# Attention with pooled keys and a channel mix on one core: probabilities transposed in 32 by 32 blocks on VectorE and moved through device memory

## The chip, the core and the metric

One core of one Trainium2 chip runs the whole kernel in one launch. The core has TensorE (PE, matrix products, with weight loads listed apart as PEld), VectorE (DVE), ScalarE (ACT), GpSimd (POOL) and SyncE (SP, which here only issues transfers). The metric is the device time of one launch in microseconds; smaller is better.

## The reference

```python
# attention: q, k, v are [8, 8, 576, 64]; keys and values are means over groups of 8
k_p = k.reshape(B, H, Sp, pool, D).mean(axis=3)          # Sp = 72
v_p = v.reshape(B, H, Sp, pool, D).mean(axis=3)
scores = scale * np.matmul(q, k_p.transpose(0, 1, 3, 2))
scores = scores - np.max(scores, axis=-1, keepdims=True)
attn = np.exp(scores)
attn = attn / (np.sum(attn, axis=-1, keepdims=True) + 1e-09)
x = np.matmul(attn, v_p)       # then heads side by side: x is [8, 576, 512]
# channel mix
x_prev = np.concatenate([np.zeros((B, 1, D)), x[:, :-1, :]], axis=1)   # D = 512
xk = mu_k * x + (1.0 - mu_k) * x_prev
xr = mu_r * x + (1.0 - mu_r) * x_prev
k = np.maximum(xk @ w_k, 0.0)                            # w_k [512, 1024]
v = k * k @ w_v                                          # w_v [1024, 512]
r = 1.0 / (1.0 + np.exp(-(xr @ w_r)))                    # w_r [512, 512]
return r * v
```

All is float32, and the result is [8, 576, 512].

## The kernel before

The 8 x 576 = 4608 tokens are cut into 12 chunks of 384 and each chunk into three tiles of 128, 36 tiles in all. A batch is one and a half chunks. Every part of the work is a Python generator (a thread): `softmax(i)` for a tile, `transposed(i)` and `transposed_rest(c, first, n)` for the transposes of its probabilities, `attended(c, g, p)` for the product with the values of head pair g (four pairs), `x_parts` for the split of the mixed inputs, `hidden(c, jt, p)` for eight blocks of the first product, `gate(c, tt)` and `mixed(c, tt)` for three tiles of the other two.

From chunk 1 on products are made of three products of split operands: each operand is rounded to a shorter type (its high part, names ending in h) and the difference is kept as a low part (ending in l); high times high, low times high and high times low are added. In chunk 0 weights and inputs are used whole. The weights arrive with eight bytes per number, in `got_wk`, `got_wr` and `got_wv` (eight, four and eight blocks of 512 KB), and `convert` makes 32-bit numbers of them: L510 on ScalarE, then a pass for the last bits, L513 on ScalarE or L518 on VectorE as `LAST_BITS_BY` says, then L523 and L526 on VectorE. `split` (L539 on ScalarE, L542 on VectorE or GpSimd by `LOW_BY`) makes the parts for the chunks behind the first.

A tile's probabilities go this way: scores of two heads at a time (L670, bank `sc`, 128 tokens by 8 heads by 72 keys); row maximum (L685); subtraction and exponential (L703, L708, sum in L710), or for the tiles of `BY_HEAD` eight exponentials with a bias and a running sum (L694); division as a product with a reciprocal, the first 64 keys of each head into `pm` (L728) and the last 8 into `px` (L722), on VectorE or GpSimd by `NORM_BY`. TensorE then transposes `pm` in four pieces (L747) and `px` in one (L774); ScalarE and VectorE copy the results out of the banks as `pth`, `ptl` and `ptr` (L755, L758, L760, L782, L785, L791). `attended` multiplies (L833). ScalarE scales the product into `t` (L840), GpSimd carries the token before a chunk (L847, L849, L851), VectorE mixes (L860, `xm`), ScalarE rounds (L876: `xkh`, `xrh`) and GpSimd subtracts (L878: `xkl`, `xrl`). Then come `hidden` (L905 and the squares L917 to L932), `gate` (L956, L963) and `mixed` (L988, L1002), and the output (L1004).

The order of the instructions is made before the run: class `Order` steps through all threads, keeps for each engine the time at which it is free by a table of costs, and of the threads whose next step could start takes the one with the smallest due time. Due times come from formulas (`FIRST`, `PER_TOKEN`, `tile_due`, `att_due`) and, where the table `DUE` names a thread, from that. Each engine then runs its own list in that order, and waits where an operand or a buffer isn't ready. All transfers but one are in SyncE's list.

`SUM_BY` says who adds the eight members of a group: "v" VectorE and "g" GpSimd by halving (L550), "t" TensorE by eight matmuls with the identity (L561, `summed`).

Of the kernel before, what the change touches and what calls it, by code (L numbers as in the profile page):

```python
# [21 lines left out]
KM = 64  # L22
# [19 lines left out]
    "k1 k0 q0 wk1 q1 v0 q2 wk5 v1 c0 v2 k3 wk0 r0 wr3 k2 wk2 wk7 q5 q3 wk6 v3 wv7 q4 wk4 wk3 "  # L42
    "wv6 wv3 wr1 r1 wv1 wv4 wv2 wv0 wr2 wv5 wr0 "
)

SUM_BY = {"k0": "v", "k1": "v", "v0": "v", "v1": "t", "r0": "t", "k2": "t", "k3": "v", "v2": "g", "v3": "g", "r1": "g", "k5": "g", "k4": "v", "v5": "v", "r2": "g", "v4": "g"}

NORM_BY = {0: "v", 1: "g", 2: "v", 3: "v", 7: "v", 5: "g", 4: "g", 8: "g", 6: "g"}
# [3 lines left out]
LAST_BITS_BY = {"k": "aaaaavaa", "r": "aava", "v": "aaaavaav"}  # L52
LOW_BY = {"k": "vgvgvvvv", "r": "vvgv", "v": "gvvvggvg"}
BY_HEAD = (0, 1, 5, 6)
# [2 lines left out]
SQUARED_ON_ACT = 7
# [1045 lines left out]
```

## Time and profile before

| | us |
|---|---|
| median of 3 runs (lowest, highest) | 641.22 (638.55, 642.38) |
| profiled execution, its own time | 642.0 |
| its span, first to last instruction | 640.1 |
| TensorE busy | 618.4 (97%), 3188 matmul records |
| VectorE, ScalarE, GpSimd busy | 380.7, 371.8, 211.2 |
| granted TensorE clock, mean | 0.99 |
| moved by DMA | 50.91 MB |

Busy times are unions over the span; lines of the form L905 are lines of the kernel before. In the rows below, `x704` counts records, the two numbers behind the bar are busy microseconds and mean nanoseconds of one record, and what follows the second bar is idle time of the engine ahead of them and what ended it. A float32 matmul of whole operands shows as two records. Records of TensorE overlap, so the time of a run of matmuls is read from the chain of work, not from the mean. A row of windows names a stretch, its length, the busy time of PE, PEld, DVE, ACT and POOL with counts, the granted clock, the share of the DMA engines and GB/s.

### The profile page before, as it was taken

The page shows a single profiled execution, that of the slowest core. Times are in us where ns is not written, and L with a number is a line of the kernel's source. Part 1 is how long each engine was busy: PE and PEld are TensorE (multiplying, and loading weights), DVE is VectorE, ACT ScalarE, POOL GpSimd, SP SyncE. Part 2 cuts the span into 40 slices and gives each one's busy share as a digit, 9 for nine tenths or more (in the row PEclk, how much of TensorE's full clock was granted, in tenths as well). Part 3 has the DMA queues.
Part 4 walks back from the last instruction along what each step waited for, and adds up shares of the span by engine and source line. Part 5 has one row for each costly group of instructions (what it writes and reads, how often), then busy time and mean ns, then how long its engine had stood idle before and what let it go on. Part 6 is the DMA issues. An engine that isn't in the chain of part 4 may idle for free.

```text
span 640.1 us, 8886 instructions
## 1 busy us (share of the span) xinstructions
PE 618.4 (97%) x3188; PEld 534.3 (83%) x3188; DVE 380.7 (59%) x723; ACT 371.8 (58%) x761; POOL 211.2 (33%) x327
## 2 busy tenths in 40 slices
PE   5898988999999999999999999999999999999997
...
GB/s 315 356 355 91 123 39 103 34 112 135 1 33 50 1 198 65 18 93 138 17 17 54 30 180 51 34 18 33 141 107 50 34 2 33 17 1 33 17 1 50
DMA packets 35132, 50.91 MB, mean 80 GB/s; under 512 B 6544, under 2 KB 23184, under 8 KB 35088
## 3 DMA queue, kind: packets, MB, share of 16 engines
...
q10 hardware_dynamic: 144, 0.13, 0.1%
...
## 4 chain that ended last, share of the span: by engine, by line
PE 83%; ACT 2%; POOL 0%; DVE 0%; issue 0%; DVEq 0%
PE mm L905 29%; PE mm L988 28%; PE mm L956 14%; PE bank L833 5%; PE sc L670 4%; PE bank L747 2%; ACT t L840 1%; PE bank L774 1%; ACT e L694 0%; POOL xkl L878 0%; ACT L694 0%; ACT got_wv L513 0%; ACT w_k L539 0%; ACT kbd L586 0%; POOL xrl L878 0%
## 5 line engine op out<-in xcount | busy, mean ns | idle before, releaser
L905 PE MATMUL mm<-xkh,w_k 128*128 128x384 f32 x704 | 181.6, 338 | 0.0
L988 PE MATMUL mm<-w_v,sh 128*128 128x512 f32 x528 | 171.1, 393 | 0.0
L905 PEld LDWEIGHTS mm<-xkh,w_k 128*128 128x128 f32 x704 | 126.0, 188 | 1.6 <-issue 1.4
L905 PE MATMUL mm<-xkl,w_k 128*128 128x384 f32 x352 | 117.9, 335 | 1.6 <-POOL xkl L878 1.6
L988 PEld LDWEIGHTS mm<-w_v,sh 128*128 128x128 f32 x528 | 99.2, 188 | 19.5
L988 PE MATMUL mm<-w_v,sl 128*128 128x512 f32 x264 | 102.9, 390 | 0.0
L956 PE MATMUL mm<-w_r,xrh 128*128 128x512 f32 x264 | 86.2, 397 | 0.0
L840 ACT ACTIVATE t<-bank,om_sb 128x384 f32<-128x384 f32 x96 | 49.1, 583 | 55.9 <-PE bank L833 55.2
L860 DVE SCALAR_TENSOR_TENSOR xm<-bank,mu_sb,t 128x384 f32<-128x384 f32 x88 | 50.7, 614 | 48.6 <-POOL t L851 26.1
L722 POOL TENSOR_TENSOR px<-e,sm 128x64 f32<-128x64 f32 x32 | 10.6, 332 | 203.5 <-DVE sm L716 198.0
L930 ACT CAST sh<-rk 128x384 fp32r<-128x384 f32 x88 | 45.1, 514 | 45.3 <-DVE rk L924 44.3
L905 PEld LDWEIGHTS mm<-xkl,w_k 128*128 128x128 f32 x352 | 66.1, 188 | 1.9 <-POOL xkl L878 1.9
L932 DVE TENSOR_TENSOR sl<-rk,sh 128x384 fp32r<-128x384 f32 x88 | 53.1, 608 | 23.7 <-ACT sh L930 22.9
L917 ACT ACTIVATE rk<-mm 128x384 f32<-128x384 f32 x88 | 43.0, 488 | 35.8 <-PE mm L905 33.8
L1002 DVE TENSOR_TENSOR rs<-mm,rs 128x512 f32<-128x512 f32 (+1 forms) x37 | 24.9, 674 | 63.2 <-PE mm L988 63.0
L924 DVE SCALAR_TENSOR_TENSOR rk<-mm,rk 128x384 f32<-128x384 f32 x88 | 48.6, 554 | 23.0 <-ACT rk L917 22.6
L550 POOL TENSOR_TENSOR stage<-stage 128x512 f32<-128x512 f32 (+8 forms) x60 | 52.5, 888 | 24.6 <-DMA stage<-in_kT 10.4
L878 POOL TENSOR_TENSOR xkl<-xm,xkh 128x384 fp32r<-128x384 f32 x44 | 44.9, 1022 | 45.1 <-ACT xkh L876 44.7
L956 PEld LDWEIGHTS mm<-w_r,xrh 128*128 128x128 f32 x264 | 49.6, 188 | 9.9
L988 PEld LDWEIGHTS mm<-w_v,sl 128*128 128x128 f32 x264 | 49.7, 188 | 8.9
L956 PE MATMUL mm<-w_r,xrl 128*128 128x512 f32 x132 | 51.4, 390 | 0.0
L670 PE MATMUL sc<-kbd,qs 128*128 128x144 f32 (+1 forms) x312 | 41.5, 292 | 5.9 <-ACT kbd L586 3.3
...
## 6 DMA issues: line engine op xcount, KB each, us to landing
out<-rs SPq DMA_DIRECT2D x35, 256.0 KB, 2.0
...
qs<-in_qT SPq DMA_DIRECT2D x32, 256.0 KB, 3.2
...
```

Of the source, the lines that this page charges most:

```text
L550: nc_eng.tensor_tensor(out=st[:, :, :w], in0=st[:, :, :w], in1=st[:, :, w:2 * w], op=ALU.add)
L670: nc.tensor.matmul(out=halves[g // 2][o:o + n, 0, k:k + 2 * KEYS], lhsT=qs[:, g, o:o + n], rhs=kbd[b % 2][:, g, :], start=True, stop=True,)
L840: nc.scalar.activation(out=t[:, m, 1:n + 1], in_=xp, func=AF.Copy, scale=om_sb[:, m, g:g + 1])
L860: nc.vector.scalar_tensor_tensor(out=xm[:, :n], in0=xp, scalar=mu_sb[:, m, g:g + 1], in1=t[:, m, :n], op0=ALU.mult, op1=ALU.add,)
L878: nc.gpsimd.tensor_tensor(out=lo, in0=xm[:, :n], in1=hi, op=ALU.subtract)
L905: nc.tensor.matmul(out=hp, lhsT=w[:, o], rhs=x[:, ct, o_t], start=(ct == 0 and k == 0), stop=(ct == NCT - 1 and k == len(terms) - 1),)
L917: nc.scalar.activation(out=rk[:, :n], in_=hp, func=AF.Relu)
L924: nc.vector.scalar_tensor_tensor(out=rk[:, :n], in0=hp, scalar=0.0, in1=rk[:, :n], op0=ALU.max, op1=ALU.mult)
L930: nc.scalar.copy(out=sh, in_=rk[:, :n])
L932: nc.vector.tensor_tensor(out=operand("sl", c)[:, jt, o_t], in0=rk[:, :n], in1=sh, op=ALU.subtract)
L956: nc.tensor.matmul(out=bank, lhsT=x[:, ct, o], rhs=w, start=(ct == 0 and k == 0), stop=(ct == NCT - 1 and k == len(terms) - 1),)
L988: nc.tensor.matmul(out=bank, lhsT=s[:, o], rhs=w, start=(jt == 0 and k == 0), stop=(jt == NJT - 1 and k == len(terms) - 1),)
```

## The change

For the tiles of chunks 2 to 11 the transposes on TensorE are gone. `softmax` normalizes all 72 keys in place (one pass), and a new thread `turned` has VectorE transpose the tile in blocks of 32 by 32 into `pm` (two instructions of 256 elements per partition and one of 64) and writes it to device memory (`passing`, two buffers of one chunk each). `fetch_turned` reads a chunk back in five transfers into `turned_sb` so that the blocks lie where whole transposes would have put them, and `split_turned` makes `pth`, `ptl` and `ptr` from it, out of SBUF instead of a bank. `turned_sb` is one buffer; until the weights are converted its space serves as the four temporaries of `convert` (two before).

The other tables are written anew as well: the order of the loads, who sums, who normalizes, which exponentials go by head, where the last bits of the weights are made (ScalarE 16 blocks of 20 before, 7 now), who makes the low parts, and all due times (two leads become constants `TILE_LEAD` and `ATT_LEAD`).

```diff
 LOADS = (
-    "k1 k0 q0 wk1 q1 v0 q2 wk5 v1 c0 v2 k3 wk0 r0 wr3 k2 wk2 wk7 q5 q3 wk6 v3 wv7 q4 wk4 wk3 "
-    "wv6 wv3 wr1 r1 wv1 wv4 wv2 wv0 wr2 wv5 wr0 "
+    "k0 q3 k1 v1 q0 wr3 q1 r0 c0 wk0 q4 wk1 q2 wv6 k3 v0 k2 wk4 wr2 wv1 wr0 wk3 wk2 v3 v2 wk5 "
+    "q5 wv2 wv4 r1 wk7 wv7 wv5 wk6 wv3 wv0 wr1 "
 )
-SUM_BY = {"k0": "v", "k1": "v", "v0": "v", "v1": "t", "r0": "t", "k2": "t", "k3": "v", "v2": "g", "v3": "g", "r1": "g", "k5": "g", "k4": "v", "v5": "v", "r2": "g", "v4": "g"}
-NORM_BY = {0: "v", 1: "g", 2: "v", 3: "v", 7: "v", 5: "g", 4: "g", 8: "g", 6: "g"}
+SUM_BY = {"k0": "t", "k1": "t", "v0": "t", "v1": "t", "r0": "t", "k2": "t", "k3": "t", "v2": "v", "v3": "g", "r1": "v", "k5": "v", "k4": "v", "v5": "v", "r2": "v", "v4": "v"}
+NORM_BY = {0: "g", 1: "g", 2: "v", 3: "g", 7: "v", 5: "v", 4: "g", 8: "v", 6: "v"}
-LAST_BITS_BY = {"k": "aaaaavaa", "r": "aava", "v": "aaaaavaav"}
-LOW_BY = {"k": "vgvgvvvv", "r": "vvgv", "v": "gvvvggvg"}
-BY_HEAD = (0, 1, 5, 6)
+LAST_BITS_BY = {"k": "aaavvavv", "r": "vavv", "v": "vavvvavv"}
+LOW_BY = {"k": "gvvvvvvv", "r": "vvvg", "v": "vgvvvgvv"}
+BY_HEAD = (0, 4, 8)
-SQUARED_ON_ACT = 7
+SQUARED_ON_ACT = 8
+TURNED = 2
+BLOCK = 32
 DUE = {
...
-    "attended 1 0 0": 8.52, "attended 1 1 0": 42.01, "attended 1 2 0": -16.71, "attended 1 3 0": -45.79,
+    "attended 1 0 0": -189.68, "attended 1 1 0": -34.56, "attended 1 2 0": -32.08, "attended 1 3 0": 49.09,
...
-PER_TOKEN = 0.131
+PER_TOKEN = 0.1331
+TILE_LEAD = -7.9807
+ATT_LEAD = 20.4607
...
-    slots("pm", 2, [P, 2, 4, KM])
+    slots("pm", 2, [P, 2 * 4 * KEYS])
...
-    slots("tmp", 2, [P, WP])
+    turned_sb = const.tile([P, CH // BLOCK, 6 * BLOCK], F32, name="turned_sb")
+    for i in range(4):
+        order.give("tmp", turned_sb.rearrange("p a n -> p (a n)")[:, i * WP:(i + 1) * WP])
+    passed = ctx.enter_context(tc.tile_pool(name="passed", bufs=1, space=bass.MemoryType.DRAM))
+    passing = [passed.tile([CH // P, P, 18 * BLOCK], F32, name=f"passing{i}") for i in range(2)]
...
-        begin[c - 1] + 5 + 0.042 * o if c > 1 else (begin[0] + SECOND + 0.03 * o if c else o / P) for c, o, _ in tiles
+        begin[c - 1] + TILE_LEAD + 0.042 * o if c > 1 else (begin[0] + SECOND + 0.03 * o if c else o / P) for c, o, _ in tiles
...
-    att_due = [b - 24 if c else 0 for c, b in enumerate(begin)]
+    att_due = [b - ATT_LEAD if c else 0 for c, b in enumerate(begin)]
...
         eng = nc.vector if v else nc.gpsimd
+        if tiles[i][0] >= TURNED:
+            yield dve(8 * KEYS) if v else pool(8 * KEYS)
+            eng.tensor_tensor(out=e, in0=e, in1=sm.broadcast_to([P, 2, 4, KEYS]), op=ALU.mult)
+            order.give("sm", sm)
+            yield from turned(i, e)
+            return
...
+    def turned(i, e):
+        c, off, _ = tiles[i]
+        u = yield take("pm")
+        yield "dve", 0.9, False
+        pairs = e.rearrange("p a (h two) k -> p (a h) two k", two=2)
+        for h2 in range(2):
+            nc.vector.transpose(
+                out=u[:, h2 * 8 * BLOCK:(h2 + 1) * 8 * BLOCK].rearrange("p (f g j) -> p f g j", f=2, j=BLOCK),
+                in_=pairs[:, :, h2, :KM].rearrange("p g (f j) -> p f g j", j=BLOCK),
+            )
+        nc.vector.transpose(
+            out=u[:, 16 * BLOCK:].rearrange("p (r h k) -> p r h k", r=2, k=KR), in_=e[:, :, :, KM:]
+        )
+        order.give("e", e)
+        if c - 2 >= TURNED:
+            yield need(("turned", c - 2))
+        yield "sp", 0.6, False
+        nc.sync.dma_start(out=passing[c % 2][off // P], in_=u)
+        order.fetched(("passed", i), 450)
...
+    def fetch_turned(c):
+        n = CHUNKS[c] // P
+        yield need(*[("passed", i) for i, t in enumerate(tiles) if t[0] == c])
+        d = yield take("turned")
+        yield "sp", 3.0, False
+        from_dram = passing[c % 2][:n].rearrange("t (a i) m -> i (t a) m", i=BLOCK)
+        for q in range(4):
+            nc.sync.dma_start(
+                out=d[q * BLOCK:(q + 1) * BLOCK, :n * 4, :4 * BLOCK],
+                in_=from_dram[:, :, q * 4 * BLOCK:(q + 1) * 4 * BLOCK],
+            )
+        nc.sync.dma_start(out=d[:BLOCK, :n * 4, 4 * BLOCK:], in_=from_dram[:, :, 16 * BLOCK:])
...
+    def split_turned(i):
+        c, off, _ = tiles[i]
+        yield need(("turned", c), ("attended", c - 1))
...
+        nc.scalar.copy(out=pt_h, in_=main)
+        nc.scalar.copy(out=ptr[:rows], in_=rest)
+        nc.vector.tensor_tensor(out=pt_l, in0=main, in1=pt_h, op=ALU.subtract)
+        nc.vector.tensor_tensor(out=ptr[rows:2 * rows], in0=rest, in1=ptr[:rows], op=ALU.subtract)
+        nc.scalar.copy(out=ptr[2 * rows:], in_=rest)
...
+        if tiles[i][0] >= TURNED:
+            order.add(tile_due[i] + 0.1, split_turned(i), spare)
+            continue
```

What stands where changes on every engine. Three places are shown. The first is TensorE where chunk 6 begins: the end of the last `mixed` tile of chunk 5 (weights `w_v`), the scores of a tile (`sc`), and `hidden` of chunk 6 (`w_k`). Before, the four matmuls of the last `attended` group stand 21 matmuls of `mixed` further up:

```order
L988 MATMUL mm_117<-w_v_759,sh_2492 128x512
L988 MATMUL mm_117<-w_v_759,sl_2527 128x512
L988 MATMUL mm_117<-w_v_759,sh_2492 128x512
L670 MATMUL sc_111<-kbd_69,qs_103 128x144 x4
L905 MATMUL mm_115<-xkh_2754,w_k_426 128x384 x2
L905 MATMUL mm_115<-xkl_2755,w_k_426 128x384
```

Now, on the same engine and at the same place, the last `attended` group (L932, the old L833) has moved behind `mixed`:

```order
L1087 MATMUL mm_118<-w_v_1024,sl_2575 128x512
L1087 MATMUL mm_118<-w_v_1024,sh_2538 128x512
L932 MATMUL bank_115<-pth_2662,vbd_h_71 128x384
L932 MATMUL bank_115<-pth_2662,vbd_l_73 128x384
L932 MATMUL bank_115<-ptl_2663,vbd_h_71 128x384
L932 MATMUL bank_115<-ptr_2664,vbd_r_75 128x384
L692 MATMUL sc_114<-kbd_70,qs_107 128x144 x4
L1004 MATMUL mm_120<-xkh_2814,w_k_490 128x384 x2
L1004 MATMUL mm_120<-xkl_2815,w_k_490 128x384
```

Behind these rows the first two blocks of `hidden` alternate: three quarters of the first, one quarter of the second, then the last quarter of the first, which is the first to use the group just shown.

The second place is SyncE's list in an even chunk: query loads (`qs`) and outputs (`out`), and before nothing else but the loads of keys and values:

```order
L1004 DMA out<-rs_78 128x512
L1004 DMA out<-rs_77 128x512
L1004 DMA out<-rs_79 128x512
L469 DMA qs_104<-in_qT 128x4x128
L469 DMA qs_102<-in_qT 128x4x128
```

Now SyncE's list has the three writes of a chunk (`passing`) among them, and its five reads (`turned_sb`) behind the last write:

```order
L783 DMA passing_104<-pm_90 128x576
L491 DMA qs_106<-in_qT 128x4x64 x2
L1103 DMA out<-rs_77 128x512
L783 DMA passing_104<-pm_89 128x576
L1103 DMA out<-rs_78 128x512
L1103 DMA out<-rs_79 128x512
L491 DMA qs_107<-in_qT 128x4x128
L783 DMA passing_104<-pm_90 128x576
L799 DMA turned_sb<-passing_104 32x12x128 x4
L803 DMA turned_sb<-passing_104 32x12x64
```

A write waits there for VectorE's transposes of its tile, and what stands behind it waits too.

The third place is ScalarE in the start, where weights are converted between other work of chunk 0 (`sh` is the squared hidden layer). Before, each L510 is followed by an L513 of the same block:

```order
L510 ACTIVATE tmp_101<-got_wk_241 128x512
L614 CAST vbd_h_71<-rs_77 128x256
L513 ACTIVATE got_wk_241<-got_wk_241 128x512
L510 ACTIVATE tmp_100<-got_wk_245 128x512
L513 ACTIVATE got_wk_245<-got_wk_245 128x512
L917 ACTIVATE sh_425<-mm_115 128x384
```

Now three of four blocks there (L532 is the old L510, L535 the old L513) have no second pass on ScalarE:

```order
L532 ACTIVATE turned_sb<-got_wk_325 128x512
L532 ACTIVATE turned_sb<-got_wv_241 128x512
L829 CAST pth_473<-bank_116 128x4x128
L535 ACTIVATE got_wv_241<-got_wv_241 128x512
L1016 ACTIVATE sh_489<-mm_119 128x384
L532 ACTIVATE turned_sb<-got_wk_347 128x512
L1020 ACTIVATE sh_489<-sh_489 128x384
L532 ACTIVATE turned_sb<-got_wv_357 128x512
```

On VectorE those passes are L540, beside the L545 and L548 of each block.

More of the change, by code (lines that the diff above doesn't have):

```diff
@@ L41 @@
 LOADS = (
[L42 to L48 removed]
+    "k0 q3 k1 v1 q0 wr3 q1 r0 c0 wk0 q4 wk1 q2 wv6 k3 v0 k2 wk4 wr2 wv1 wr0 wk3 wk2 v3 v2 wk5 "
+    "q5 wv2 wv4 r1 wk7 wv7 wv5 wk6 wv3 wv0 wr1 "
+)
+SUM_BY = {"k0": "t", "k1": "t", "v0": "t", "v1": "t", "r0": "t", "k2": "t", "k3": "t", "v2": "v", "v3": "g", "r1": "v", "k5": "v", "k4": "v", "v5": "v", "r2": "v", "v4": "v"}
+NORM_BY = {0: "g", 1: "g", 2: "v", 3: "g", 7: "v", 5: "v", 4: "g", 8: "v", 6: "v"}
 WARMING = 4
 FILLS = ((("scored", 1), 0),)
[L52 to L54 removed]
+LAST_BITS_BY = {"k": "aaavvavv", "r": "vavv", "v": "vavvvavv"}
+LOW_BY = {"k": "gvvvvvvv", "r": "vvvg", "v": "vgvvvgvv"}
+BY_HEAD = (0, 4, 8)
 BESIDE = (1,)
[L57 removed]
+SQUARED_ON_ACT = 8
 REST_BY = (1, 1, 3)
+TURNED = 2
+BLOCK = 32
 DUE = {
[46 rows of a table removed]
[58 rows of a table added]
+    "split_turned 7": 50.64, "split_turned 8": 127.66, "split_turned 9": 109.36, "free_turned": 15.32,
+    "fetch_turned 2": 66.88,
 }
@@ L413, in warm @@
         yield "dve", 0.5, False
-        nc.vector.memset(zeros, 0.0)
+        nc.vector.memset(zeros[:, :256], 0.0)
         bank = yield take("bank")
@@ L511, in convert @@
         if LAST_BITS_BY[kind][i] == "a":
-            yield "act", 0.57, False
+            yield "act", 1.3, False
             nc.scalar.activation(
@@ L716, in softmax @@
         nc.vector.reciprocal(out=sm, in_=sm)
-        px = yield take("px")
-        pm = yield take("pm")
         v = NORM_BY.get(i, "g") == "v"
         eng = nc.vector if v else nc.gpsimd
+        if tiles[i][0] >= TURNED:
[4 more added lines that the diff above has]
+            return
+        px = yield take("px")
+        got = yield take("pm")
+        pm = got[:, :8 * KM].rearrange("p (a h k) -> p a h k", a=2, h=4)
         yield dve(8 * KR) if v else ("pool", 0.24, True)
@@ L732, in softmax, with free_turned @@
         order.give("sm", sm)
-        held["pm", i] = pm
+        held["pm", i] = got, pm
         order.make(("pm", i))
+    def turned(i, e):
[17 more added lines that the diff above has]
+        order.fetched(("passed", i), 450)
+        order.now += 2.7
+        order.give("pm", u)
+    def free_turned():
+        yield need(*[("full", kind, i) for kind, n in (("k", NJT), ("r", NCT), ("v", NJT)) for i in range(n)])
+        order.give("turned", turned_sb)
+    def fetch_turned(c):
[10 more added lines that the diff above has]
+        nc.sync.dma_start(out=d[:BLOCK, :n * 4, 4 * BLOCK:], in_=from_dram[:, :, 16 * BLOCK:])
+        held["turned", c] = d, n
+        order.fetched(("turned", c), 1300)
     def transposed(i):
@@ L741, in transposed @@
             yield need(("early", "ptl", 0))
-        pm = held.pop(("pm", i))
+        got, pm = held.pop(("pm", i))
         bank = yield take("bank")
@@ L751, in transposed @@
             )
-        order.give("pm", pm)
+        order.give("pm", got)
         yield act(NPAIR * P)
@@ L764, in transposed @@
         order.make(("main", i))
+    def split_turned(i):
+        c, off, _ = tiles[i]
+        yield need(("turned", c), ("attended", c - 1))
+        whole_d = held["turned", c][0]
+        d = whole_d[:, off // BLOCK:(off + P) // BLOCK]
+        split_by = lambda t: t.rearrange("p g (a j) -> p g a j", j=BLOCK)
+        o = slice(off, off + P)
+        main = d[:, :, :4 * BLOCK].rearrange("p a (g j) -> p g a j", j=BLOCK)
+        rest = d[:4 * KR, :, 4 * BLOCK:].rearrange("p a (r j) -> p r a j", j=BLOCK)
+        pt_h, pt_l = split_by(operand("pth", c)[:, :, o]), split_by(operand("ptl", c)[:, :, o])
+        ptr, rows = split_by(operand("ptr", c)[:, :, o]), 4 * KR
+        yield act(NPAIR * P)
+        nc.scalar.copy(out=pt_h, in_=main)
+        yield act(2 * P)
+        nc.scalar.copy(out=ptr[:rows], in_=rest)
+        yield dve(NPAIR * P)
+        nc.vector.tensor_tensor(out=pt_l, in0=main, in1=pt_h, op=ALU.subtract)
+        order.make(("main", i))
+        yield dve(2 * P)
+        nc.vector.tensor_tensor(out=ptr[rows:2 * rows], in0=rest, in1=ptr[:rows], op=ALU.subtract)
+        yield act(2 * P)
+        nc.scalar.copy(out=ptr[2 * rows:], in_=rest)
+        left = held["turned", c][1] - 1
+        held["turned", c] = whole_d, left
+        if not left:
+            order.give("turned", whole_d)
+        order.make(("side", i))
     def transposed_rest(c, first, n):
@@ L1043, in attention_then_channel_mix @@
             order.add(tile_due[last] + 0.1, transposed_rest(c, i, n), spare)
+    order.add(-5, free_turned())
     for c, n in enumerate(CHUNKS):
+        if c >= TURNED:
+            order.add(tile_due[n // P * c + n // P - 1] + 0.05, fetch_turned(c))
         for g in range(NPAIR):
```

102 rows, old and new, of the table DUE are left out of this document.

## Prediction

> **What bounds the kernel now.** I read the busy times in five stretches first, because the page's 97% for TensorE (PE) mixes a start with a long even part. Columns: stretch, its length, then busy time of PE, weight load, VectorE (DVE), ScalarE (ACT) and GpSimd (POOL), granted clock, DMA share.
>
> ```profile
> 0.00:28.40 28.40, 19.39 (x96) 17.25 (x97) 19.06 (x47) 18.82 (x64) 6.23 (x14) 0.88 0.96 332
> 28.40:62.70 34.30, 30.54 (x120) 18.88 (x119) 28.84 (x56) 30.55 (x57) 9.37 (x17) 0.95 0.72 246
> 62.70:107.30 44.60, 39.94 (x135) 20.73 (x133) 30.77 (x58) 42.36 (x98) 16.03 (x26) 1.00 0.26 85
> 107.30:594.60 487.30, 487.26 (x2639) 440.84 (x2640) 290.27 (x544) 270.19 (x526) 178.80 (x270) 1.00 0.18 58
> ```
>
> From 107.3 to 594.6 us TensorE is never idle (487.26 of 487.30) and its clock is full: there each microsecond taken off TensorE is a microsecond off the time, as long as nothing else becomes late. Before 107.3 it idles 17.4 us, and from 62.7 on ScalarE is the full engine (42.36 of 44.60). The chain of work that ended last, in order of time, shows what TensorE does around one chunk boundary (start, length, what):
>
> ```profile
> 320.74 7.53 PE mm L956 x33
> 328.26 0.33 PE bank L774 x3
> 328.59 0.70 PE mm L956 x3
> 329.29 0.44 PE bank L747 x4
> 329.73 5.47 PE mm L988 x24
> ...
> 343.45 0.70 PE bank L833 x4
> 344.15 4.76 PE mm L988 x21
> 348.92 0.98 PE sc L670 x8
> 349.90 10.43 PE mm L905 x60
> ...
> 384.25 0.98 PE sc L670 x8
> ```
>
> **The transposes that go.** Tiles 6 to 35, thirty of them, lose four TensorE transposes each (L747, 0.44 us per tile), and ten chunks lose their three remainder transposes (L774, 0.33 us per chunk): 30 x 0.44 + 10 x 0.33 = 16.5 us. All stand behind 107.3. This is the main term.
>
> **What takes their place.** VectorE gets three block transposes per tile, two of 256 elements per partition and one of 64. No row shows such a transpose. The nearest by size and the dearest by rate are
>
> ```profile
> L616 DVE TENSOR_TENSOR vbd_l<-rs,vbd_h 128x256 fp32r<-128x256 f32 x2 | 0.8, 420 | 0.0
> L728 DVE TENSOR_TENSOR pm<-e,sm 128x512 f32<-128x512 f32 x4 | 4.9, 1225 | 0.0
> L703 DVE TENSOR_TENSOR e<-sc,mx 128x576 f32<-128x576 f32 x32 | 24.1, 754 | 1.0
> ```
>
> so from 2 x 0.42 + 0.21 = 1.05 us to 576/512 x 1.225 = 1.4 us per tile; I take 1.05, the row of that size: 3.2 us per chunk of about 48, on an engine that is 60% busy there (290.27 of 487.30). The copies and subtractions that split the result (pth, ptl, ptr) stay in number of elements. Cost at nothing; the cover is 19 us of VectorE idle per chunk, and a transpose four times as dear would still fit.
>
> Each tile is then written to device memory (288 KB) and each chunk read back in five transfers with pieces of 512 and 256 bytes. Nearest rows, with the median from issue to landing last, and below them the start of a normalization whose scores began at 384.25:
>
> ```profile
> out<-rs SPq DMA_DIRECT2D x35, 256.0 KB, 2.0
> qs<-in_qT SPq DMA_DIRECT2D x32, 256.0 KB, 3.2
> 393.62 0.29 POOL L722 TENSOR_TENSOR px<-e,sm 128x64 f32<-128x64 f32 x1 [0.34 <-DVE sm L716]
> ```
>
> The write is like the output, 2 to 3 us. The query loads move 512-byte pieces too; 864 KB at their rate is 3.4 x 3.2 = 11 us, and 4 to 5 us if the five overlap; I take 5, with 3 and 11 as ends. The last tile of chunk c+1 is scored as chunk c begins; its probabilities are used at the first L833 of chunk c's L988 stage, some 17 us of L905 (96 of them), 8 of L956 and 5 of L988 later, 30 us. From scores to normalization one tile took 9.4 us (384.25 to 393.62); normalization, block transpose, write, read and split add about 1 + 1 + 3 + 5 + 4, the split at six copies and subtractions of 0.6: 23 us, or 29 with the read at 11. So it is hidden, by 1 to 7 us at least. On SyncE's queue a write waits for VectorE and a read for the last write; behind them stand query loads and outputs, which have tens of microseconds too.
>
> **What is late next at the boundary.** Before, the last L833 of a chunk (343.45) stood 21 L988 matmuls ahead of the next L905. Now nothing but the scores stands between them, as the order rows of the change show. The work from there to the operand xkl of the fourth block is this, each of the first six rows starting as the one before ends (the timeline of each engine, L833 first; then the xkl of the next L833 group, and a group row):
>
> ```profile
> 342.44 0.34 PE L833 MATMUL bank<-ptr,vbd_r 96*128 96x384 f32 x1
> 342.87 1.05 ACT L840 ACTIVATE t<-bank,om_sb 128x384 f32<-128x384 f32 x2 [2.10 <-PE bank L833]
> 343.99 0.18 POOL L849 COPY carry<-t 128x2 f32<-128x2 f32 x1 [1.48 <-ACT t L840]
> 344.24 1.14 DVE L860 SCALAR_TENSOR_TENSOR xm<-bank,mu_sb,t 128x384 f32<-128x384 f32 x2 [1.44 <-POOL t L851]
> 344.89 0.51 ACT L876 CAST xkh<-xm 128x384 fp32r<-128x384 f32 x1 [0.97 <-DVE xm L860]
> 345.49 1.02 POOL L878 TENSOR_TENSOR xkl<-xm,xkh 128x384 fp32r<-128x384 f32 x1 [1.28 <-ACT xkh L876]
> 347.95 1.01 POOL L878 TENSOR_TENSOR xkl<-xm,xkh 128x384 fp32r<-128x384 f32 x1
> L550 POOL TENSOR_TENSOR stage<-stage 128x512 f32<-128x512 f32 x12 | 16.1, 1343 | 8.6 <-DMA stage<-in_vm 8.6
> ```
>
> From 342.78 to 346.51 is 3.7 us. In that time TensorE now has the scores (0.98) and 14 to 20 hidden matmuls of 0.174 (10.43/60): 3.4 to 4.5 us; at the last boundary, without scores, 3.0. In four of ten boundaries it falls short by 0.3 to 0.8; VectorE's score reduction and GpSimd's sums (1.34 us for the first pass), which now stand in between in some chunks, can add 1 us. I take 3 us in all, from 0 to 9 (ten boundaries of 0.9).
>
> **The start.** Rows that price it:
>
> ```profile
> L513 ACT ACTIVATE got_wk<-got_wk 128x512 uint16<-128x512 uint16 x7 | 9.5, 1355 | 0.1
> L518 DVE TENSOR_SCALAR got_wv<-got_wv 128x512 uint16<-128x512 uint16 x2 | 1.9, 940 | 0.2 <-ACT tmp L510 0.2
> L542 DVE TENSOR_TENSOR w_k<-got_wk,w_k 128x512 fp32r<-128x512 f32 x6 | 4.2, 704 | 0.0
> L694 ACT ACTIVATE e<-sc,mx 128x72 f32<-128x72 f32 x24 | 7.3, 330 | 1.7 <-PE mm L670 1.7
> 4.69 3.10 DVE L550 TENSOR_TENSOR stage<-stage 128x576 f32<-128x576 f32 x6 [2.14 <-DMA stage<-in_kT]
> L561 PE MATMUL mm<-stage,ident 128*128 128x144 f32 x16 | 2.1, 286 | 0.0
> 8.51 2.29 PE L670 MATMUL sc<-kbd,qs 128*128 128x144 f32 x8 [3.27 <-ACT kbd L586]
> L561 PE MATMUL mm<-early_sl,ident 128*128 128x128 f32 x16 | 3.6, 421 | 0.0
> 48.00:52.00 4.00, 2.06 (x5) 0.97 (x4) 3.49 (x10) 3.33 (x6) 0.69 (x2) 0.86 1.02 346
> 52.00:56.00 4.00, 4.00 (x13) 2.36 (x12) 2.84 (x4) 2.03 (x5) 1.36 (x1) 0.71 0.06 15
> ```
>
> ScalarE loses nine L513 passes (9 x 1.355 = 12.2 us) and one net exponential by heads (2.6 less one pass of 0.7). VectorE gains nine passes of up to 0.94 (8.5), three splits (2.1), sums for v2 and r1 (3.1, at 3.10/2 each), two more softmax passes of 0.75, and tile 6's work brought forward (four such passes and a transpose, 4.1); it loses the sums of k0, k1, k3 and v0 (6.2): +13 us on 78.7, so about 92. It has next to nothing to do before the first scores are done, which I put at 11 us: they began at 8.51, after 3.10 us of sums for k0 and k1 on VectorE, and now two sums of 2.1 on TensorE and a query load stand ahead of them. So even without a gap its queue reaches the end of this stage at 102: ScalarE's limit goes, VectorE's stands close behind. TensorE gains four sums of 2.1 us, in the first 28 us, where it idles 9.
>
> DMA is full to 52 us and the order of loads now puts a block of w_r last. The first L956 needs all of w_r, so it can't start before about 54; VectorE's queue has some 50 us of work ahead of that block, from 11 on, which gives 61 against 62.7. After that TensorE needs its 39.9 us, idle 4.66 before. I take 2 us from the first part and 2 of the 4.66: **4 us gained**, from 8 lost (VectorE late in every step) to 12 gained (54 instead of 62.7, and most of the idle time).
>
> One clock effect: the sum at 18.8 us (early_sl) took 3.6 us, a later one of more columns 2.1. The new k sums follow the warm-up matmuls directly. The Trainium skill, "TensorE: Matmul & The Clock Gate", section "Part 1: The HAM clock gate", has the array at half clock until about 3.4 us of sustained work; by that rule both k sums run at 2.1 us and the first scores are about as early as before, by the slow row they are 3 us later, and my sum would be 3 us more. The trace agrees as far as its slow records are the early ones.
>
> **The sum.** 640.1 - 16.5 + 3 - 4 = 622.6 us of span; the profiled execution took 642.0, 1.9 more than its span, so 624.5. Its time stands 0.8 above the median 641.22, so about **624** there.
>
> **Rivals.**
> 1. *The boundary takes more.* If the work queued on ScalarE, VectorE and GpSimd in front of xkl is late by 1 to 2 us at each of ten boundaries, the time is 631 to 638. For it: the two L833 groups in a row, as at 342.07 and 343.45, already make the second xkl end (348.96) 4.8 us after its matmuls (344.15). Against: one group alone has 3.7.
> 2. *The start gains more.* ScalarE was at 95% for 45 us; if VectorE's new passes fall in its idle time the start gains 8 to 12: 616 to 620.
> 3. *The start loses.* VectorE, 92 us of work in order, waits for loads as it did and reaches 115: 8 lost, 636; with rival 1, no change.
> 4. *The round trip is late.* A read that lands after the 30 us stops TensorE once in each of ten chunks. It decides from a read of about 15 us; each microsecond beyond costs 10 in all, so at 20 us the time is 674, slower. For it: pieces of 256 and 512 bytes into 32 partitions at a time, which no row shows. Against: 3.2 us for the query loads' 512-byte pieces. The Trainium skill, "VectorE: DVE Perf Modes", section "The three transpose paths", warns that a plain strided DMA copy used for a transpose is 19 times slower than the crossbar one when the innermost stride is large; here the innermost runs are whole 256 and 512 bytes, so the trace's row stands nearer.
> 5. *It doesn't do what it says.* The transposes of chunks 0 and 1 stay on TensorE; the order has none behind them, so I give this nothing.
>
> **How the numbers follow.** Forecast (616 to 631) 0.60; start gains more 0.13; boundary 0.12; start loses 0.07; round trip late 0.08. A measurement here can tell about 1%, 634.8 and 647.6. Faster: 0.60 + 0.13 + two thirds of the boundary case = 0.81; same: 0.04 of the boundary case and 0.07 of the lost start = 0.11; slower: 0.08, the late round trip. Leaving out 2 in 10, the range goes from 611 (a start at its best end, no boundary stalls) to 637.
>
> **What would show it.** No L747 or L774 after the second chunk; TensorE near 100% busy between the start and the last chunk, with idle time only before xkl; first continuous L905 at 100 to 105; VectorE at 65%; the block transpose near 0.42 us; the reads landing in about 5 us. Wrong if TensorE waits before L833 (round trip), or if VectorE is above 95% up to the second chunk.

## The result: 635.9 us, 0.7% faster

| | before | changed |
|---|---|---|
| median (lowest, highest) | 641.22 (638.55, 642.38) | 635.91 (634.81, 637.72) |
| ratio, 95% interval | | 0.9929 (0.9906 to 0.9951) |
| profiled execution, its span | 642.0, 640.1 | 636.05, 634.2 |
| TensorE busy | 618.4 | 609.6 |
| VectorE, ScalarE, GpSimd busy | 380.7, 371.8, 211.2 | 404.6 (64%), 360.9, 187.8 |

The change gained 5.3 us where 17 were forecast, and it stays within the 1% (634.8 to 647.6) that the prediction called the same. The same stretches of the changed kernel as in the first rows of the prediction:

```profile
0.00:28.40 28.40, 21.61 (x146) 19.05 (x147) 15.19 (x38) 15.75 (x45) 4.76 (x13) 1.00 0.96 316
28.40:62.70 34.30, 31.68 (x133) 19.56 (x132) 33.66 (x72) 31.09 (x75) 6.90 (x15) 1.00 0.87 302
62.70:107.30 44.60, 43.78 (x164) 25.95 (x163) 39.28 (x77) 33.05 (x68) 13.70 (x22) 1.00 0.21 69
107.30:594.60 487.30, 476.72 (x2492) 427.79 (x2491) 306.69 (x638) 272.77 (x558) 162.49 (x230) 0.99 0.33 93
```

Up to 107.3 us TensorE idles 10.2 us, where it idled 17.4. From there on it was never idle before; now it is idle for 10.6 us (487.30 - 476.72). Its waits, with their sum, their number and the longest:

```profile
PE mm L1004 <- ACT rs L1062: 5.7, 1, 5.7
PE mm L1004 <- POOL xkl L977: 3.3, 8, 0.5
```

One wait of 5.7 us and eight of up to 0.5, all on L1004, the old L905: the first block of `hidden`, at a chunk boundary. To place them I divide the span at marks that both kernels have: the start of the last `mixed` matmul of a chunk (L988, now L1087) in TensorE's records. The forecast's row is its sum laid over the marks: 1.65 us of transposes per chunk (chunk 2's lie ahead of the first mark), 0.3 us per boundary, and 4 for the start.

| us | to the end of chunk 1 | chunks 2 and 3 | chunks 4 to 11 | rest | span |
|---|---|---|---|---|---|
| before | 154.0 | 99.2 | 382.2 | 4.6 | 640.1 |
| forecast | 148.4 | 96.5 | 373.1 | 4.6 | 622.6 |
| changed | 147.7 | 105.8 | 376.5 | 4.2 | 634.2 |

The start came about as forecast. Of the 11.6 us that are missing, 9.2 were lost in chunks 2 and 3 and 3.5 in the eight chunks behind, and 1.1 came back in the first and last stretch. The marks don't enclose the same work in every order: two groups of four matmuls of the product with the values, 0.70 us each, stand behind the end of chunk 3 in the changed kernel and ahead of it before. For the same work the two losses are nearer to 10.6 and 2.1.

**The wait before chunk 3.** The chain of work of the changed kernel there (start, length, what):

```profile
195.31 0.70 PE bank L932 x4
196.00 1.38 PE mm L1055 x6
197.99 1.95 POOL xrl L977 x2
199.94 0.95 POOL xkl L977
202.25 0.95 ACT t L939 x2
204.15 7.99 PE mm L1004 x30
```

and ScalarE's timeline (start, length, what, and in brackets its idle time and what ended it):

```profile
197.40 0.51 ACT L975 CAST xrh<-xm 128x384 fp32r<-128x384 f32 x1 [6.09 <-PE mm L1055]
197.82 0.51 ACT L975 CAST xkh<-xm 128x384 fp32r<-128x384 f32 x1
198.65 1.04 ACT L939 ACTIVATE t<-bank,om_sb 128x384 f32<-128x384 f32 x2
201.74 0.51 ACT L975 CAST xkh<-xm 128x384 fp32r<-128x384 f32 x1 [2.05 <-DVE xm L959]
202.16 1.05 ACT L939 ACTIVATE t<-bank,om_sb 128x384 f32<-128x384 f32 x2
203.50 0.60 ACT L1062 ACTIVATE rs<-mm 128x512 f32<-128x512 f32 x1
```

Six matmuls of chunk 2's `gate` (L1055) stand behind the last product with the values (L932). They read `xrh`, of which there is one buffer, so ScalarE's cast of chunk 3 into `xrh` waits for them until 197.40. Everything for chunk 3 stands behind that cast in ScalarE's list: the casts of the second and third head pair (197.82, 201.74), the scaling of the third and fourth (198.65, 202.16), and the sigmoid (203.50) that frees the bank TensorE waits for. The products of the first two pairs had been done since 189 us.

**The other boundaries.** VectorE, ScalarE, GpSimd and TensorE at the start of chunk 6:

```profile
351.50 0.76 DVE L707 TENSOR_REDUCE mx<-sc 128x8 f32<-128x576 f32 x1 [0.99 <-PE sc L692]
352.18 0.61 DVE L959 SCALAR_TENSOR_TENSOR xm<-bank,mu_sb,t 128x384 f32<-128x384 f32 x1
352.82 0.52 ACT L975 CAST xkh<-xm 128x384 fp32r<-128x384 f32 x1 [1.19 <-DVE xm L959]
353.42 1.01 POOL L977 TENSOR_TENSOR xkl<-xm,xkh 128x384 fp32r<-128x384 f32 x1 [1.50 <-ACT xkh L975]
354.48 0.45 PE L1004 MATMUL mm<-xkl,w_k 128*128 128x384 f32 x1 [0.47 <-POOL xkl L977]
```

This is what the prediction described: the score reduction stands in front of the mix, and `xkl` is late by 0.5 us.

The new parts cost what was forecast. The block transposes (two groups of the changed kernel), then its writes and reads (KB and median us to landing):

```profile
L772 DVE STREAM_TRANSPOSE pm<-e 128x256 f32<-128x256 f32 x60 | 23.0, 422 | 17.6 <-POOL e L743 17.6
L776 DVE STREAM_TRANSPOSE pm<-e 128x64 f32<-128x64 f32 x30 | 6.1, 202 | 0.0
```

```profile
passing<-pm SPq DMA_DIRECT2D x30, 288.0 KB, 2.1
turned_sb<-passing SPq DMA_DIRECT2D x40, 192.0 KB, 4.5
```

### The profile page after: what moved, and what is told of

The parts are those of the page before. It is cut to its first block, busy times and chain, and to the rows that moved or that the text cites. A ratio compares the mean times of both kernels' runs of the same rounds, so it can differ in the third digit from the quotient of the medians.

```text
span 634.2 us, 8948 instructions
## 1 busy us (share of the span) xinstructions
PE 609.6 (96%) x3102; PEld 523.5 (83%) x3102; DVE 404.6 (64%) x838; ACT 360.9 (57%) x758; POOL 187.8 (30%) x280
## 4 chain that ended last, share of the span: by engine, by line
PE 75%; DVE 7%; POOL 6%; ACT 5%; DMA 4%; issue 2%; SPq 1%; DVEq 0%; POOLq 0%; ACTq 0%
PE mm L1087 26%; PE mm L1004 25%; PE mm L1055 15%; PE bank L932 4%; PE sc L692 4%; POOL xkl L977 2%; DMA qs<-in_qT 2%; POOL xrl L977 2%; DVE xm L959 2%; DMA turned_sb<-passing 1%; POOL stage L572 1%; ACT xkh L975 1%; ACT t L939 1%; DVE mx L707 1%; DVE got_wk L548 0%
## 5 line engine op out<-in xcount | busy, mean ns | idle before, releaser
L1004 PE MATMUL mm<-xkh,w_k 128*128 128x384 f32 x704 | 183.3, 341 | 8.1 <-ACT rs L1062 5.7
L1087 PE MATMUL mm<-w_v,sh 128*128 128x512 f32 x528 | 169.8, 391 | 0.0
L1004 PEld LDWEIGHTS mm<-xkh,w_k 128*128 128x128 f32 x704 | 127.5, 190 | 11.0 <-ACT rs L1062 5.9
L1004 PE MATMUL mm<-xkl,w_k 128*128 128x384 f32 x352 | 119.6, 340 | 3.3 <-POOL xkl L977 3.3
L1087 PEld LDWEIGHTS mm<-w_v,sh 128*128 128x128 f32 x528 | 99.2, 188 | 20.0 <-ACT ptr L851 0.4
L1087 PE MATMUL mm<-w_v,sl 128*128 128x512 f32 x264 | 102.9, 390 | 0.0
L743 POOL TENSOR_TENSOR e<-e,sm 128x576 f32<-128x576 f32 x27 | 32.4, 1199 | 190.1 <-DVE sm L738 156.1
L1055 PE MATMUL mm<-w_r,xrh 128*128 128x512 f32 x264 | 84.4, 393 | 0.0
L1004 PEld LDWEIGHTS mm<-xkl,w_k 128*128 128x128 f32 x352 | 66.9, 190 | 5.8 <-POOL xkl L977 5.8
L1031 DVE TENSOR_TENSOR sl<-rk,sh 128x384 fp32r<-128x384 f32 x88 | 51.1, 592 | 12.1 <-ACT sh L1029 11.1
L1055 PEld LDWEIGHTS mm<-w_r,xrh 128*128 128x128 f32 x264 | 49.6, 188 | 10.1
L1016 ACT ACTIVATE rk<-mm 128x384 f32<-128x384 f32 x88 | 42.8, 490 | 25.2 <-PE mm L1004 15.2
L1087 PEld LDWEIGHTS mm<-w_v,sl 128*128 128x128 f32 x264 | 49.6, 188 | 9.1
L1055 PE MATMUL mm<-w_r,xrl 128*128 128x512 f32 x132 | 51.4, 389 | 0.0
L977 POOL TENSOR_TENSOR xrl<-xm,xrh 128x384 fp32r<-128x384 f32 x44 | 45.1, 1026 | 11.0 <-ACT xrh L975 10.8
L975 ACT CAST xkh<-xm 128x384 fp32r<-128x384 f32 x44 | 22.5, 514 | 38.4 <-DVE xm L959 38.1
```

Of the source, the lines that this page charges most:

```text
L743: eng.tensor_tensor(out=e, in0=e, in1=sm.broadcast_to([P, 2, 4, KEYS]), op=ALU.mult)
L975: nc.scalar.copy(out=hi, in_=xm[:, :n])
L977: nc.gpsimd.tensor_tensor(out=lo, in0=xm[:, :n], in1=hi, op=ALU.subtract)
L1004: nc.tensor.matmul(out=hp, lhsT=w[:, o], rhs=x[:, ct, o_t], start=(ct == 0 and k == 0), stop=(ct == NCT - 1 and k == len(terms) - 1),)
L1016: nc.scalar.activation(out=rk[:, :n], in_=hp, func=AF.Relu)
L1031: nc.vector.tensor_tensor(out=operand("sl", c)[:, jt, o_t], in0=rk[:, :n], in1=sh, op=ALU.subtract)
```

## The experiments

Each was timed beside the kernel before, whose medians there were 639.0 to 640.1, so ratios are the measure. The last five columns are the stretches of the one traced execution, between the marks used above; it can lie at an end of the run's spread (627.5 for gate and lead, 646.2 for the new tables with PE transposes, the lowest and the highest of their launches). Work moves over the mark between chunks 3 and 4 from order to order, so the sum, 2 to 11, is the safer figure: 481.4 in the kernel before, 482.3 in the changed kernel, 469.6 in the forecast. Up to the end of chunk 1 the changed kernel and the first nine rows have as many matmuls of scores and of the product with the values as the kernel before; in the last six up to 16 of them stand on the other side of that mark.

| | median us | ratio (95%) | to chunk 1 | 2 and 3 | 4 to 11 | 2 to 11 | span |
|---|---|---|---|---|---|---|---|
| changed, again | 635.61 | 0.9947 (0.9930 to 0.9965) | 147.9 | 105.1 | 376.4 | 481.5 | 633.7 |
| gate on time | 633.25 | 0.9905 (0.9883 to 0.9927) | 149.3 | 101.6 | 375.2 | 476.8 | 630.3 |
| lead alone | 633.62 | 0.9910 (0.9890 to 0.9930) | 148.4 | 106.9 | 371.9 | 478.8 | 631.4 |
| gate and lead | 631.99 | 0.9893 (0.9869 to 0.9917) | 147.1 | 103.7 | 370.6 | 474.3 | 625.7 |
| gate and lead, again | 631.62 | 0.9869 (0.9847 to 0.9892) | 150.1 | 104.8 | 370.6 | 475.4 | 629.8 |
| gate and split | 630.17 | 0.9853 (0.9829 to 0.9878) | 147.6 | 99.0 | 376.0 | 475.0 | 626.9 |
| all three | 627.17 | 0.9809 (0.9787 to 0.9830) | 150.7 | 100.7 | 370.3 | 471.0 | 626.0 |
| all three, sums on GpSimd | 640.38 | 1.0013 (0.9998 to 1.0028) | 163.5 | 100.6 | 370.3 | 470.9 | 638.7 |
| kept warm | 635.52 | 0.9935 (0.9915 to 0.9955) | 148.7 | 103.7 | 376.5 | 480.2 | 633.2 |
| new tables, PE transposes | 643.12 | 1.0060 (1.0041 to 1.0079) | 156.6 | 98.8 | 384.8 | 483.5 | 644.4 |
| gate and lead, from chunk 3 | 628.17 | 0.9841 (0.9814 to 0.9868) | 152.9 | 100.5 | 368.5 | 468.9 | 626.1 |
| all three, from chunk 3 | 630.39 | 0.9848 (0.9823 to 0.9873) | 155.8 | 100.9 | 368.7 | 469.6 | 629.7 |
| old tables | 636.73 | 0.9953 (0.9937 to 0.9969) | 153.0 | 107.5 | 370.1 | 477.6 | 634.9 |
| old tables, from chunk 3 | 629.17 | 0.9837 (0.9811 to 0.9863) | 151.4 | 97.4 | 372.5 | 469.9 | 625.5 |
| the same, later split | 627.95 | 0.9811 (0.9788 to 0.9834) | 151.8 | 97.6 | 371.4 | 469.0 | 625.0 |

### The gate tile on time

```diff
 DUE = {
-    "gate 2 1": 220.95,
```

> Only the due time of the second gate tile of chunk 2 (220.95) is taken out of the table, so its last six matmuls stand with the others, ahead of the 72 matmuls of mixed. Theory A (the late gate): those six matmuls release the buffer of xrh at 197.4 us, in ScalarE's list the whole split of chunk 3 stands behind the cast into it, and TensorE stood still for 5.7 us and then ran 6.8 us at half clock. Without it both go: 5.7 + up to 3.4, so 627 to 630 us. Theory B (the stall is the split of chunk 3 itself, too much work behind the last product with the values, whatever the gate does): most of the stall stays, 633 to 636.

633.25 us. The wait of 5.7 us and the half clock are gone from the trace, and chunks 2 and 3 take 101.6 instead of 105.8. So the late gate tile is the cause of that wait. But not all of it came back. TensorE's waits at the same boundary now:

```profile
207.82 0.44 PE L1004 MATMUL mm<-xkl,w_k 128*128 128x384 f32 x1 [1.02 <-POOL xkl L977]
209.91 0.62 PE L1004 MATMUL mm<-xkh,w_k 128*128 128x384 f32 x2 [0.58 <-DVE rk L1023]
```

Theory A was right on the mechanism and its 627 to 630 was missed by 3 us: other work was late next.

### The products with the values earlier

```diff
-ATT_LEAD = 20.4607
+ATT_LEAD = 24.0
```

together with the gate tile on time:

> As the one before, and ATT_LEAD 24 instead of 20.46, which puts 21 to 24 matmuls of mixed behind the last product with the values of each chunk from chunk 3 on. Theory A (each later boundary waits 0.4 to 0.65 us for xkl because nothing but scores covers the split): those seven waits go, 4.5 us, so 4 to 5 us below the run before, 623 to 625. Theory B (the waits come from a backlog on GpSimd and VectorE at these places, sums and score reductions, not from where the product stands): no more than 1 us gained.

631.99 us, 1.3 below the run without it where 4 to 5 were expected. By the columns chunks 4 to 11 fell by 4.6 and chunks 2 and 3 rose by 2.1, but about half of the fall and all of the rise is work that changed columns. Scores (L692) and products with the values (L932) between the marks of chunks 2 and 3, in the run with the gate on time and then in this one (stretch, length, busy time and number of matmuls, then of weight loads):

```profile
149.30:250.92 101.62, 8.06 (x64) 7.53 (x64) 1.00 0.40 107
149.30:250.92 101.62, 7.36 (x44) 6.54 (x44) 1.00 0.40 107
147.13:250.85 103.72, 9.20 (x72) 8.64 (x72) 1.00 0.39 107
147.13:250.85 103.72, 8.35 (x52) 7.38 (x52) 1.00 0.39 107
```

Eight more of each, 2.4 us at the chain's 0.98 for eight scores and 0.70 for four of the product. Over chunks 2 to 11 the lead gains 2.5 (476.8 to 474.3). The waits around the start of chunk 3 didn't go. VectorE, ScalarE and TensorE of this run there:

```profile
199.29 2.40 DVE L572 TENSOR_TENSOR stage<-stage 128x576 f32<-128x576 f32 x3
201.62 1.13 DVE L959 SCALAR_TENSOR_TENSOR xm<-bank,mu_sb,t 128x384 f32<-128x384 f32 x2
216.85 1.14 ACT L849 CAST pth<-turned_sb 128x512 fp32r<-128x512 f32 x2 [2.09 <-DMA turned_sb<-passing]
219.04 0.47 ACT L1016 ACTIVATE rk<-mm 128x384 f32<-128x384 f32 x1
220.83 0.50 PE L1055 MATMUL mm<-w_r,xrh 128*128 128x512 f32 x1 [1.62 <-DVE rk L1023]
```

Sums of keys stand in front of the mix (199.29), and ScalarE's cast waits 2.09 us for the chunk that is read back, with L1016 behind it, for which TensorE then waits 1.62 us. In the run with the gate on time TensorE waits 1.21 us at the same place.

The same kernel once more, and the lead alone beside the changed kernel:

> The run with the gate on time and the earlier products once more, unchanged, for its spread (627.5 to 636.1 before, with a profile at its lower end). Theory A (ScalarE's cast waits for a read whose landing varies from launch to launch, with the rectified blocks behind it): again a spread of several microseconds and a median of 631 to 633. Theory B (the spread was chance): a median of 626 to 629 as the profile has it, and the later split is worth nothing.

631.62 us (629.86 to 632.36): the median repeated, the spread of 8.7 us did not. Between its two traces lie 4.1 us, of which 3.0 arose before the end of chunk 1, by launch.

> The changed kernel with ATT_LEAD 24 instead of 20.46 and nothing else: the late gate tile of chunk 2 stays where it is, behind the last product with the values, and from chunk 4 on the products stand 18 to 24 matmuls of mixed earlier. Theory A (the boundaries behind chunk 3 cost about 5 us in all, as the traces with and without the lead say, 375.6 and 370.4 us from the end of chunk 3 to the end of chunk 11): 5 us below the changed kernel, 630 to 632. Theory B (the loss is the one wait before chunk 3): 634 to 637.

> The changed kernel once more, unchanged. Theory A (the wait before chunk 3 follows from the order alone): the same wait of 5 to 6 us before the first hidden matmul of chunk 3, a half clock behind it, 635 to 637. Theory B (it was an accident of one launch): no such wait in the trace, 629 to 632 in some launches.

The wait before chunk 3 is 5.66 us, to the hundredth, in all three traces that leave the gate tile late and the gap empty, and each time half clock follows; so it comes from the order. The lead alone gave 633.62 against 635.61, 2.0 us. Again eight scores and eight matmuls of the product changed columns, which is why chunks 4 to 11 fall by 4.6 and chunks 2 and 3 rise by 1.8; over chunks 2 to 11 the gain is 2.7 (481.5 to 478.8). So the boundaries behind chunk 3 cost 2 to 3 us and not theory A's 5, and the wait before chunk 3 is still there: the loss has two places, and both theories hold in part.

### The split of the chunk that is read back, later

```diff
-        order.fetched(("turned", c), 1300)
+        order.fetched(("turned", c), 1300 if c == 2 else 2300)
```

With the two edits above, and with the gate tile alone:

> The run with the earlier products, and the schedule reckons with 2300 KB in place of 1300 KB for reading a chunk back from chunk 3 on, so ScalarE's list has the casts into pth later. Theory A (in that run the cast waited for the read until 216.85 us with the rectified blocks behind it, and TensorE lost 1.9 us at 220.8): the wait goes, 1 to 3 us less, 629 to 631. Theory B (the waits come from VectorE's and ScalarE's load there, not from the read): no change, 631 to 633.

627.17 us (627.13 to 627.93), better than either theory said, and the best of all kernels. ScalarE no longer waits for a read, and chunks 2 and 3 take 100.7, where the two traces without this edit and with the same number of scores and products there have 103.7 and 104.8.

> The run with the gate tile on time, and the later split of the chunks that are read back (2300 KB reckoned from chunk 3 on), ATT_LEAD as in the changed kernel. Theory A (the early split was worth most of the 5 us between the runs with and without it): 628 to 630, and the boundary waits for xkl that the earlier products take away are worth the 1 to 2 us between this run and the one with all three. Theory B (the earlier products and the later split only help together): 632 to 634.

630.17 us, theory A within 0.2. With the lead as well the time is 3.0 lower, and chunks 2 to 11 take 471.0 in place of 475.0.

### The clock behind the wait

```diff
+            if (c, jt, ct) == (3, 1, 0):
+                other = min(order.slots["bank"], key=lambda h: h[0])[1]
+                for _ in range(24):
+                    nc.tensor.matmul(out=other[:, :P], lhsT=ident, rhs=ident, start=True, stop=True)
```

> The changed kernel with 24 products of the identity with itself put on TensorE between the scores and the first hidden matmul of chunk 3, into a free bank that nothing reads, so TensorE works through most of the 5.7 us in which it waits there. The wait itself stays. Theory A (the idle time costs twice, since TensorE ran the next 6.8 us at half clock): the clock stays full there and the time falls by 2 to 3.4 us, 632.5 to 634. Theory B (the half clock costs nothing, because the split of chunk 3 sets the pace behind the wait): 635 to 637.

The changed kernel first, in windows around the wait; then this run, whose fill begins at 199.9 and ends at 205.6 (the seventh number is the granted clock):

```profile
198.50:202.80 4.30, 0.00 (x0) 0.00 (x0) 1.14 (x2) 2.25 (x6) 3.02 (x6) 1.00 0.24 61
202.80:209.60 6.80, 5.45 (x17) 5.45 (x18) 4.47 (x7) 4.79 (x8) 3.67 (x6) 0.50 0.10 39
```

```profile
199.90:205.60 5.70, 5.61 (x50) 5.42 (x48) 1.75 (x4) 3.62 (x8) 4.23 (x9) 1.00 0.18 46
205.60:212.40 6.80, 6.77 (x41) 6.77 (x42) 5.30 (x12) 4.78 (x8) 3.29 (x4) 1.00 0.11 41
```

TensorE starts 17 matmuls in the 6.8 us at half clock, from which it waits another 1.35, and 41 in 6.8 us when it was kept busy. Chunks 2 and 3 took 103.7 us against 105.8 and 105.1. So in the trace the half clock cost 1.4 to 2.0 us. The median, 635.52 against 635.91 and 635.61, is theory B's, and the ratios' intervals lie over each other. Whether the clock costs anything in the time as measured stays open.

### The tables and the path apart

The old path with the new tables, without the late gate tile (`TURNED = 99`), and the new path with the tables of the kernel before:

> The new tables alone, without the late gate tile: all transposes stay on TensorE. Theory A (transposes are worth 16.4 us on a full engine): 16 above the run with the gate on time, 642 to 646, so the new tables are worth nothing by themselves: 6 us gained in the start, some microseconds lost at the boundaries. Theory B (the transposes were half hidden and are worth some 8 us): 634 to 638.

643.12 us, in theory A's range, but not by its sum: it set this run 16 above the run with the gate on time, which was itself expected lower than it came. That run (633.25) differs from this one in the path alone and is 9.9 us faster, nearer to theory B's 8. By the traces 9.6 us of the difference lie in chunks 4 to 11 (384.8 to 375.2), which have the same number of scores and products in both; there seven chunks have 11.55 us of transposes, and TensorE waits 1.3 us more without them. The run with all three edits, which has the lead and the split besides, is 16 us faster; what the lead does with the new tables on the old path was not measured.

> The new path alone: block transposes and device memory from chunk 2 on, with all tables of the kernel before (loads, sums, due times; two temporaries). Theory A (removing the transposes is worth their 16.4 us where the product with the values stands early enough; the loss came with the new tables): 641 - 16.4 and something for the start of chunk 1 and 2, where the products with the values now fall between the hidden blocks, 625 to 629. Theory B (the new path itself costs TensorE about 10 us, by waits behind the round trip or by crowded ScalarE and VectorE): 633 to 638.

636.73 us, theory B's number, and yet theory A's mechanism (L990 is the L1004 of the others): chunks 4 to 11 take 370.1, about as in the best run, and the loss lies in chunks 2 and 3 (107.5). Of the 10.1 us that these take more than in the next run, some 3.4 are 24 scores and products that stand elsewhere there; most of the rest are TensorE's waits, 4.1 us against 0.9, and two stretches at half clock. The old order brings chunk 2's scores too late for the longer way; its products with the values then stand between blocks of `hidden`, and TensorE waits there:

```profile
157.46 0.62 PE L990 MATMUL mm<-xkh,w_k 128*128 128x384 f32 x2 [1.67 <-ACT xkh L961]
169.21 0.44 PE L990 MATMUL mm<-xkl,w_k 128*128 128x384 f32 x1 [1.93 <-POOL xkl L963]
```

Leaving chunk 2 on TensorE (`TURNED = 3`) avoids that:

> All tables of the kernel before, the new path from chunk 3 on (chunk 2's transposes stay on TensorE). Nine chunks lose 1.635 us each, 14.7. Theory A (the path costs nothing in the even part, and the run with the old tables lost its gain only where chunk 2 begins, since its tiles come too late for the longer way): 640.5 - 14.7, and at most 2 us of stalls, 625.5 to 628. Theory B (the round trip or the crowding costs something in every chunk): 631 to 636.

629.17 us, 1.2 above theory A's range, and 7.6 below the run with chunk 2 turned. With the later split as well:

> The run with the old tables and the new path from chunk 3 on, and the later split. Theory A (the early split costs there too): 627 to 628.5, 1 to 2 below the run without it, and less spread. Theory B (in that order the split stood late enough): 628.5 to 630, no change.

627.95 us, in theory A's range, though the interval reaches the run before it. So the old tables with the new path end where the new tables end. The same two runs with the new tables:

> The run with the earlier products, with chunk 2's transposes left on TensorE: 1.6 us more of TensorE work, and 6 block transposes, three writes and five reads less before 160 us. Theory A (the early turned tiles crowd ScalarE and VectorE where chunks 2 and 3 begin, some 4 us of stalls): 629 to 631. Theory B (the early tiles cost nothing): 633 to 635.

628.17 us, below theory A's range and 3.5 to 3.8 below the two runs that turn chunk 2: by the medians turning it costs more than it saves without the later split, though the interval reaches that of the second of the two.

> The run with the new tables (gate on time, earlier products) and the new path from chunk 3 on, and the later split. Theory A (the early turned tiles of chunk 2 are worth their 1.6 us): 628 to 629, above the run with chunk 2 turned as well. Theory B (they cost what they bring): 625.5 to 627.5, at or below it.

630.39 us, neither range: by these medians chunk 2's turned tiles gain 3.2 us with the later split, where they lost 3.5 without it. The traces don't explain that. The end of chunk 1 comes at 155.8 here and at 152.9 in the run before, though the order on every engine is the same in both up to 159 us, so 2.9 us are the launch; and of the 5.1 us to the best run's 150.7, 3.3 are chunk 2's transposes and 12 scores and products that stand ahead of the mark here. What turning chunk 2 is worth with the new tables stays open.

### Sums back on GpSimd

```diff
-"v2": "v", "r1": "v", "k5": "v", "r2": "v", "v4": "v"
+"v2": "g", "r1": "g", "k5": "g", "r2": "g", "v4": "g"
```

> The run with all three edits, and five sums (v2, r1, k5, r2, v4) back on GpSimd, as the kernel before has them. Theory A (what is left around chunks 2 and 3 is VectorE's sums, up to 2.4 us in front of the mix of a boundary): 1 to 3 us less, 624.5 to 626.5. Theory B (GpSimd's sums, 1.3 us for the first pass, then stand in front of xkl instead): 627 to 630.

640.38 us; both theories miss. Chunks 2 and 3 (100.6) and all behind are as they were, so what is left there doesn't come from these sums. The whole loss is in the start, 12.8 us to the end of chunk 1: the schedule writes ScalarE's list otherwise, with passes over the weights (L535, L532) in front of an L1016 that frees a bank, and TensorE waits. Up to the end of chunk 1 it is idle for 19.4 us in place of the best run's 10.4, and the wait shown here (ScalarE's timeline, then TensorE's) is 5.5 of them; the others were not followed:

```profile
63.67 1.33 ACT L535 ACTIVATE got_wv<-got_wv 128x512 uint16<-128x512 uint16 x1
65.29 0.67 ACT L532 ACTIVATE turned_sb<-got_wv 128x512 f32<-128x512 f32 x1
67.40 0.49 ACT L1016 ACTIVATE sh<-mm 128x384 f32<-128x384 f32 x1
67.95 7.42 PE L1055 MATMUL mm<-got_wr,xrh 128*128 128x512 f32 x11 [5.53 <-ACT sh L1016]
```

## Why the prediction was wrong, step by step

- **What bounds the kernel: right.** TensorE's work and waits make the time in every run.
- **The transposes, 16.5: right as a price.** With the new tables chunks 4 to 11 are 9.6 us shorter without the transposes (384.8 to 375.2) and have 1.3 us more of waits, where seven chunks of 1.65 make 11.55.
- **What takes their place: right.** Block transposes 0.422 and 0.202 us (0.42 and 0.21 forecast), writes 2.1 us, reads 4.5 (5). The longest wait of ScalarE for a read, 1.3 us in the changed kernel, did not reach TensorE there; with the gate tile on time it did, by 1.21 us, and with the lead besides by 1.62. Rival 4 was a matter of where the split stands in ScalarE's list, not of 15 us of reading.
- **The start, 4 gained: about right, by luck in part.** First scores at 11.04 us (11 forecast), sums of keys 2.2 us (2.1), first L1055 at 60.50 (61), VectorE busy 88.1 us up to 107.3 (92). The end of chunk 1 came 6.3 earlier, 5.65 forecast. But the old order varies by 2.6 us there (154.0, 151.4, 151.8 with chunk 2 on TensorE) and the new one by 3.6 (147.1 to 150.7); from mean to mean it is 3.8, of which 1.65 are transposes, so some 2 us of start.
- **The boundary, +3 with a range of 0 to 9: the step that failed.** It priced one path, from the last product to `xkl`, and took it ten times. That path came as priced: eight waits for `xkl`, 3.3 us in all. But chunks 2 to 11 take 482.3 us, where the kernel before without its transposes there (481.4 less nine times 1.65) would take 466.6: 15.7 us in place of 3. What the step left out is other work at the same place, before chunk 3 above all. A reader of `xrh` that the new order put behind the product costs the wait of 5.7 us and the half clock behind it (5.5 us by the traces with and without it, 2.4 to 2.7 by the medians); the early split costs 3.1 to 4.8 by the medians. The earlier products, which cover the priced path, bring 1.3 to 3.0. With all three edits chunks 2 to 11 take 471.0, 1.4 above the forecast. The prediction reckoned with nothing but scores between the product and L1004 and showed chunk 6; the six matmuls of L1055 stand before chunk 3 alone.
- **Rival 1, the boundary takes more, chance 0.12: its time came, by luck.** 635.9 lies in its 631 to 638, but it had `xkl` late by 1 to 2 us at each of ten boundaries, and in the changed kernel TensorE waited for none of them longer than 0.5. By its own condition, 10 to 20 us in place of 3, its upper end should have been 641.
- **The clock.** The slow row of the first sums didn't return: the sums of keys took 2.2 us in both traced executions. What the clock does in the start differs from launch to launch: it is 1.00 up to 62.7 us in the one shown and half from 14.7 to 18.1 us in the other. In the kernel before it was half from 16.7 to 23.6 us, where the slow sum stands. At the wait before chunk 3 it fell in both. The Trainium skill, "TensorE: Matmul & The Clock Gate", section "HAM oscillation — how this bites in real kernels", has idle gaps of more than about 3.4 us throttle the array. The trace agrees: half clock from 202.8, 4.3 us after the last matmul.

The best run is 3 us above the forecast, 627.2 against 624. In its trace the end of chunk 1 comes at 150.7, where 148.4 was forecast, and chunks 2 to 11 take 471.0 in place of 469.6. Its 100.7 in chunks 2 and 3, 4.2 above the forecast, hold 16 score matmuls, 2.0 us, that stand behind chunk 3 in the kernel before (72 against 56 here, 152 against 168 in chunks 4 to 11), and 1.2 us of waits. The cause of the remaining 1 us was not found; moving five sums to GpSimd did not change it.
